# Gated linear attention and eight experts on one core: the second product of experts 3 to 7 by Strassen's seven products, in steps of 256 tokens

## The chip, the cores and the metric

The kernel runs on one NeuronCore of a Trainium2 chip. The metric is the time of one execution on the device, in microseconds (us); less is better. The kernel before took 1843.33 us, the median of three runs (1843.16 to 1844.97).

Engines are named as in the profile: PE does matrix products (PEld is its weight load), DVE and ACT do elementwise work, POOL does elementwise work on SBUF only, SP issues most DMAs. PE writes only to PSUM; DVE and ACT read and write PSUM and SBUF.

## The reference

Two parts. A recurrent attention over 4 batches, 8 heads, 768 tokens and head size 48 gives x, 3072 tokens by 384 columns. Then eight experts work on every token, and their results are mixed with weights P:

```python
def _attn_ref(q, k, v, alpha):
    ...
    for t in range(S):
        state = alpha[:, :, t, :, None] * state + np.einsum('bhd,bhe->bhde', k[:, :, t], v[:, :, t])
        y[:, :, t] = np.einsum('bhd,bhde->bhe', q[:, :, t], state)

def _moe_ref(x, w_gate, w1, w2):
    N, D = x.shape              # 3072, 384
    E = w_gate.shape[1]         # 8, and w1 is (8, 384, 1024), w2 is (8, 1024, 384)
    logits = x @ w_gate
    logits = logits - logits.max()
    P = np.exp(logits)
    for _ in range(8):
        P /= P.sum(1, keepdims=True) + 1e-09
        P /= P.sum(0, keepdims=True) + 1e-09
        P *= N / E
    out = np.zeros((N, D), dtype=np.float32)
    for e in range(E):
        h = np.maximum(x @ w1[e], 0.0)
        ye = h @ w2[e]
        out += P[:, e:e + 1] * ye
```

Every token goes through every expert, so nothing is gathered: each expert is two dense products, 3072 x 384 x 1024 (the first product) and 3072 x 1024 x 384 (the second).

## The kernel before

**Number format.** Each operand of the experts' products is held as two f16 tensors, a high part and a low part (index 0 and 1 of `h`, `w1`, `w2`, `xT`). A product of two such operands takes three passes (`PASSES`: high x high, high x low, low x high), all added in PSUM. `split` makes the two parts: ACT scales and rounds to the high part, DVE subtracts to get the low part.

**Early stage.** The attention is done in 24 chunks of 128 tokens, prepared by 12 blocks of 256 tokens. A block is a chain that goes back and forth between POOL (products `tmp`) and DVE (sums into `AB`), and ends with a round trip through DRAM. PE has little attention work, so the experts 0, 1 and 2 (`NA = 3`) are worked on meanwhile, as filler: `moe_tile` generators are pushed on the list `filler`, 256 tokens each, as soon as the tokens' x and the expert's weights are there, and `fill(us)` advances the first one by so many estimated microseconds of PE work. The order of everything up to the eighth chunk is written out by hand in the string `START`: `c0` advances chunk 0 by one step, `b2` block 2, `w1` the weights of expert 1, `d2` the decays of unit 2, `f` calls `fill(0.45)`; a capital letter puts some of that step's work on POOL instead of DVE. A loop with `FILL` orders the rest. In this stage `hold` pins all engines to the order in which the code is written. The unweighted results of experts 0 to 2 go to DRAM (`raw`), since P is known only at the end of the attention.

**Sinkhorn.** `sinkhorn` makes P: eight rounds, each a short chain of DVE operations, a product on PE, and DVE again. What is left of the filler runs beside it, and the weights of expert 3 are loaded and split.

**Late stage.** Experts 3 to 7, one after the other, in tiles of 512 tokens, also by `moe_tile`: for each of the 8 slices f of 128 hidden units, 9 matmuls 512 columns wide, ACT's relu into the high part of h, DVE's relu-and-subtract into the low part; then for each of the 4 token tiles of 128, 24 matmuls 384 columns wide into one PSUM tile, which `evac_add` multiplies by P and adds to `acc`. For expert 3 `evac_first` first reads the three `raw` results of that token tile back (`ri`) and adds them. While expert e runs, `load_expert(e + 1)` loads and splits the next weights, one step for each step of `moe_tile`. The products are pinned in their order by `mm`; DVE, ACT and SP are ordered by the framework's scheduler here. PSUM tiles: `psm` (4 banks), `psa` (2) and `psb` (2), all kept to the end.

The lines that matter: `PASSES` and `moe_tile`, `load_expert`, `fill` and `filler`, `sinkhorn`, and the last loop over `range(NA, E)`.

Of the kernel before, what the change touches and what calls it, by code (L numbers as in the profile page):

```python
# [8 lines left out]
F16 = mybir.dt.float16  # L9
# [14 lines left out]
def tile_gla_moe(ctx: ExitStack, tc: tile.TileContext, q, k, v, alpha, wg, w1, w2, out):  # L24
    nc = tc.nc
# [13 lines left out]
    START = 'c0 c1 f c0 f f f c1 W0 w0 f f c0 f c1 f f f f f w0 c0 f f W0 w0 f f f f f f c0 f f f c1 w0 f w0 c1 c0 f f f f w1 f w0 f f w0 f f w0 c1 w0 f w0 W1 f f c0 c2 f f f c2 f c1 f g c1 c0 c3 f f c1 f f W0 c0 f W0 f w0 f c2 c3 f f c1 f c1 f W0 c0 g c2 f w1 f f c0 W1 f f c3 w1 g f f c2 W1 f c3 c2 c1 f f f c3 w1 w0 f f f c2 f f f w1 c3 f f f c2 f f f f f f f w1 c3 f f W1 c3 f w1 f f f f f f f f f c3 w1 f c2 w1 b2 w1 w1 f f f W1 f c2 f f b2 f f f f f f c2 f f f f f f B2 f w1 f B2 f c2 c3 f f f b2 f f f f c3 c3 f f f f B2 f B2 b2 f f f f f f f f B2 f f f f f f f f f f f f f b2 f f b2 f f B2 B2 B2 f f f f b2 f f B2 f f f f f f f f f f f f f f f f c4 d2 f f f f f c4 f f f B3 b3 f f b3 c0 c4 f f f f f b3 b3 b3 b3 b3 f f f f f b3 w2 c5 f f f f f b3 f f f f f b3 w2 c4 f f f f f f b3 f f f f f b3 w2 c5 f f f f f b3 f f f f f b3 w2 c4 f f f f f f b3 f f f f f w2 c5 f f f f f f f f f f w2 d3 c6 f f f f f f f f f f f b4 w2 c5 f f f f f b4 f f f f f b4 w2 c6 f f f f f b4 f f f f f f b4 w2 c5 f f f f f b4 f f f f f b4 w2 c6 f f f f f b4 f f f f f b4 w2 c7 f f f f f f b4 f f f f f b4 w2 c6 f f f f f b4 f f f f f b4 w2 c7 f f f f f f b4 f f f f f b4 w2 c6 f f f f f b4 f f f f f w2 c7 f f f f f f f f f f f w2 d4 c8 f f f f f f f f f f b5 c7 f f f f f b5 f f f f f f b5 c8 f f f f f b5 f f f f f b5 c7 f f f f f b5 f f f f f b5'.split()  # L39
# [25 lines left out]
    def mm(out_, lhsT, rhs, start=True, stop=True):  # L65
        tc.keep_in_program_order(nc.tensor.matmul(out_, lhsT, rhs, start=start, stop=stop))  # L66
# [47 lines left out]
    def root_scale(sq, target, nm):  # L114
# [7 lines left out]
        VE.tensor_scalar_mul(p, p, 2.0 ** 64)  # L122
# [37 lines left out]
    def load_expert(e, pool, res):  # L160

        todo, pws = [], []
        for nm, w, target, C, W in (("w1", w1, W1T, KT_, FF), ("w2", w2, W2T, FT, DM)):
# [713 lines left out]
    while len(filler) > 3:  # L877
        fill(0.1)
# [65 lines left out]
```

## Time and profile before

| | |
|---|---|
| median of three runs | 1843.33 us |
| the profiled execution | 1843.05 us |
| its span, first to last instruction | 1841.3 us |
| mean granted clock of TensorE | 0.982 |
| PE busy | 1745.6 us, 14774 matmuls |
| DVE busy | 840.4 us |
| ACT busy | 541.9 us |

The profile comes from one execution. Its page gives the busy time of each engine over the whole span, and the span in 40 slices of 46 us. The views used below are: stretches (busy time of each engine in a window, with the number of instructions), groups (instructions of one shape: busy time, mean duration of one, idle time before them and what ended it), the timeline (instructions in order, equal ones merged, with idle time in square brackets), and the chain that ended last. A matmul's recorded duration includes the time to run out of the array, which the next one overlaps; its cost in a stream is the distance between the starts of groups.

### The profile page before, as it was taken

What the parts mean: (1) busy time and instruction counts of PE and PEld (TensorE: products, weight loads), DVE (VectorE), ACT (ScalarE), POOL (GpSimd) and SP (SyncE); (2) the same over time, 40 slices, a digit from 0 to 9 for tenths busy, and PEclk for the clock granted to TensorE, in tenths of its full rate; (3) what the DMA queues carried; (4) which work ended last, traced back from release to release, by engine and by line L of the source; (5) the groups of instructions that cost most, each with busy time, mean ns of one, the idle gap of its engine ahead of it and who ended that gap; (6) DMA issues with size and microseconds to landing.
All of it is one profiled execution on the core that took longest, in us unless ns stands there. A gap on an engine that the chain in (4) does not pass through costs nothing.

```text
span 1841.3 us, 34101 instructions
## 1 busy us (share of the span) xinstructions
PE 1745.6 (95%) x14774; PEld 1132.8 (62%) x14774; DVE 840.4 (46%) x1851; ACT 541.9 (29%) x1221; POOL 297.4 (16%) x270
## 2 busy tenths in 40 slices
PE   5899488999999999998999999999999999999999
PEld 5776466777777777776554555555555555555555
DVE  6465576666566556336465233222422242222222
ACT  5453243334333333325442123111411121111111
POOL 1124444445335424200000000000000000000000
PEclk9999598999999999999999999999999999999999
DMA  6114503431330432022362002000200000000000
GB/s 174 37 41 97 145 21 82 98 74 44 94 93 19 102 94 62 25 95 78 123 195 86 1 1 69 1 1 1 69 1 1 1 1 1 1 1 19 34 18 35
DMA packets 148198, 98.13 MB, mean 53 GB/s; under 512 B 107216, under 2 KB 138192, under 8 KB 148048
## 3 DMA queue, kind: packets, MB, share of 16 engines
q1 hardware_dynamic: 148048, 95.95, 18.8%
q8 instruction: 116, 1.90, 0.4%
q14 instruction: 34, 0.28, 0.1%
HBM read 67.63 MB, written 28.30 MB: 52 GB/s over the span
## 4 chain that ended last, share of the span: by engine, by line
PE 78%; DVE 10%; ACT 4%; DMA 4%; issue 2%; POOL 1%; SPq 0%; ACTq 0%; DVEq 0%; POOLq 0%
PE ps L66 70%; PE psy L66 3%; PE psl L66 2%; DMA ri<-raw 2%; DVE AB L57 2%; POOL tmp L57 1%; DVE tmp L57 1%; DVE deck L57 1%; DVE decq L57 1%; DVE h L57 1%; PE pss L66 1%; DVE w L57 1%; ACT junk L57 1%; ACT w L57 1%; ACT A L57 1%
## 5 line engine op out<-in xcount | busy, mean ns | idle before, releaser
L66 PE MATMUL ps<-xT,w 128*128 128x256 f16 (+2 forms) x4824 | 777.8, 320 | 16.8 <-DVE h L57 13.1
L66 PE MATMUL ps<-w,h 128*128 128x384 f16 x4608 | 774.1, 327 | 10.7 <-DVE h L57 9.8
L66 PEld LDWEIGHTS <-w 128*128 128x128 f16 x4824 | 467.7, 99 | 304.7 <-issue 20.1
L66 PEld LDWEIGHTS <-h 128*128 128x128 f16 x4608 | 450.0, 98 | 306.0 <-issue 9.7
L57 ACT ACTIVATE h<-ps 128x256 f16<-128x256 f32 (+2 forms) x536 | 251.6, 475 | 800.1 <-PE ps L66 799.6
L57 DVE SCALAR_TENSOR_TENSOR h<-ps,h 128x256 f16<-128x256 f32 (+2 forms) x536 | 280.9, 537 | 434.6 <-ACT h L57 434.2
L57 DVE SCALAR_TENSOR_TENSOR acc<-ps,pe,acc 128x384 f32<-128x384 f32 x120 | 74.1, 617 | 307.6 <-PE ps L66 307.6
L57 POOL TENSOR_TENSOR tmp<-qt,kt 128x768 f32<-128x768 f32 (+2 forms) x81 | 141.5, 1752 | 153.1 <-DVE AB L57 66.0
L57 DVE TENSOR_REDUCE AB<-tmp 128x16 f32<-128x768 f32 (+2 forms) x90 | 81.1, 902 | 42.0 <-POOL tmp L57 41.8
L57 ACT COPY r<-ps 128x384 f32<-128x384 f32 x72 | 34.4, 477 | 149.4 <-PE ps L66 139.7
L57 ACT COPY A<-psl 16x128 f32<-16x128 f32 (+4 forms) x164 | 52.5, 327 | 53.4 <-PE psl L66 51.9
L66 PE MATMUL psy<-vn,A 128*128 128x48 f32 x384 | 58.2, 283 | 1.7 <-issue 1.7
L66 PE MATMUL psl<-Tq,Tk 48*32 48x16 f32 (+3 forms) x2752 | 46.1, 191 | 13.9 <-DVE A L57 6.0
L66 PEld LDWEIGHTS psy<-vn,A 128*128 128x128 f32 x384 | 54.9, 209 | 2.1 <-issue 2.0
L66 PEld LDWEIGHTS psl<-Tq,Tk 48*32 48x32 f32 (+2 forms) x2752 | 40.7, 114 | 23.9 <-issue 8.7
L57 ACT ACTIVATE ys<-psy,s_t 128x384 f32<-128x384 f32 x24 | 14.0, 581 | 104.0 <-DVE s_t L57 79.4
L57 POOL TENSOR_TENSOR kt<-kt,al 128x384 f32<-128x384 f32 x40 | 41.1, 1028 | 2.6
L57 POOL TENSOR_TENSOR A<-an,mask 128x1024 f32<-128x1024 f32 x20 | 40.0, 2000 | 0.0
L57 DVE TENSOR_TENSOR qt<-qt,al 128x384 f32<-128x384 f32 (+1 forms) x50 | 39.6, 792 | 0.0
L57 DVE SCALAR_TENSOR_TENSOR acc<-ri,pe,acc 128x384 f32<-128x384 f32 x48 | 29.5, 616 | 21.4 <-DMA ri<-raw 18.3
L57 DVE TENSOR_REDUCE mx<-psy 128x1 f32<-128x384 f32 x24 | 13.3, 555 | 56.7 <-PE psy L66 56.7
L66 PE MATMUL psy<-ST,Tq 128*128 128x96 f32 x160 | 35.6, 306 | 2.9 <-DVE lg L57 1.8
(160 smaller groups left out, 965.0 us busy)
## 6 DMA issues: line engine op xcount, KB each, us to landing
raw<-r SPq DMA_DIRECT2D x72, 192.0 KB, 1.9
ri<-raw SPq DMA_DIRECT2D x72, 192.0 KB, 2.4
w1f<-in_moe_w_dram SPq DMA_DIRECT2D x5, 1536.0 KB, 6.4
w2f<-in_moe_w_dram SPq DMA_DIRECT2D x5, 1536.0 KB, 7.3
vn<-in_v_dram SPq DMA_DIRECT2D x24, 192.0 KB, 3.6
xT<-in_moe_w_dram SPq DMA_DIRECT2D x6, 768.0 KB, 6.7
out_dram<-acc SPq DMA_DIRECT2D x24, 192.0 KB, 1.9
qt<-in_q_dram SPq DMA_DIRECT2D x10, 384.0 KB, 5.4
```

What stands on the lines that cost most here:

```text
L57: r = f(*a, **k_)
L66: tc.keep_in_program_order(nc.tensor.matmul(out_, lhsT, rhs, start=start, stop=stop))
```

## The change

Three things change.

**1. The second product of experts 3 to 7.** A step is 256 tokens, that is two token tiles of 128. The second product is seen as a 2 x 2 block product: two token tiles, two halves of the hidden units (4 slices of 128 each), two halves of the output columns (192 each). Strassen's method (in Winograd's form) needs seven block products in place of eight, each 4 slices x 3 passes = 12 matmuls 192 columns wide. It needs sums of blocks: of h (four DVE operations for each of the 4 slices pairs, `hf` 4 to 7, before the split into two f16 parts, which now makes 7 x 128 = 896 columns in place of 512), and of w2 (four subtractions, once an expert, in `load_late`). Sums of the products are made in PSUM: ACT copies product X into Y, and DVE writes X + v into Z, and later products are added on top of what was written there. `acc` now takes five additions of 192 columns a step.

**2. The order of the late stage.** The seven products of a step stand between the four pieces of the next step's first product (`F` is 18 matmuls 256 columns wide). The `raw` results are read back one expert at a time: expert 0's beside expert 3, 1's beside 4, 2's beside 5. `load_late` takes the place of `load_expert`: one staging buffer in place of two (first w1, then w2), and more empty steps between its parts.

**3. The order of the early stage.** `START` is a new string: 640 entries in place of 571, 459 `f` in place of 390, `B3`, `B4` and `B5` in place of some `b3`, `b4` and `b5`. Filler left at the start of `sinkhorn` is sorted by expert, and the loading of expert 3 begins inside that part. The three PSUM pools are closed before the late stage, and two new ones opened (`psm2`, 3 banks; `psv`).

Scales of the sums of squares change by powers of two, with no new instruction.

```diff
-    START = 'c0 c1 f c0 f f f c1 W0 w0 f f c0 f c1 f f f f f w0 c0 f f W0 w0 ...'.split()
+    START = 'c0 c0 f f c1 c0 f c1 f f f f f f c1 f f W0 f f f f c0 f f f W0 W0 ...'.split()
...
+    filler[1:] = sorted(filler[1:], key=lambda x: x[0])
+    w3_ = load_late(NA)
+    advance(w3_, 1)
     for n, _ in enumerate(sinkhorn()):
         fill(2.8 if n else 4.0)
-    while len(filler) > 3:
-        fill(0.1)
+        if n > 1:
+            advance(w3_, 1)
     while filler:
-        advance(w3_, 1)
-        fill(1.0)
+        if all(e for e, _ in filler):
+            advance(w3_, 1)
+        fill(2.0)
...
+    def load_late(e):
...
+        def staged(nm, w, target):
+            t = wst.tile([P, KT_ * FF], F32, tag="wst", name=f"{nm}f_{e}")
...
+            SP.dma_start(t.rearrange("p (c f) -> p c f", f=src.shape[2]), src)
+            yield from [None] * 3
...
+                SE.activation(junk, t[:, i * n:(i + 1) * n], AF.Square, scale=2.0 ** 16, accum_out=ss[:, i:i + 1])
...
+            yield from [None] * 2
...
+        for c in range(KT_):
+            split(t[:, c * FF:(c + 1) * FF], sc, *(x[:, c] for x in w1h))
+            yield
+        t, pw2, sc = yield from staged("w2", w2, W2T)
...
+        def put(n, src):
+            split(src, sc, *(x[n // 4][:, n % 4] for x in q))
+
+        put(0, b11)
+        yield
+        VE.tensor_sub(b11, b12, b11)
+        put(3, b11)
+        yield
...
+    T = 2 * P
...
+    def first(e, t0):
...
+        for j in range(HF):
+            ps = psm.tile([P, 2, T], F32, tag="psm", name=f"ps1_{e}_{t0}_{j}")
+            for z in range(2):
+                f = j + z * HF
...
+                        mm(ps[:, z], w1h[i][:, c, f * P:(f + 1) * P], xs(k_, c, t0, T),
+                           start=(n == 0), stop=(n == 3 * KT_ - 1))
...
+            SE.activation(a[:, :4].rearrange("p (z r) t -> p z (r t)", z=2), ps, AF.Relu)
+            VE.tensor_add(a[:, 4], a[:, 0], a[:, 2])
+            VE.tensor_sub(a[:, 5], a[:, 4], a[:, 1])
+            VE.tensor_sub(a[:, 6], a[:, 1], a[:, 0])
+            VE.tensor_sub(a[:, 7], a[:, 3], a[:, 5])
+            hi, lo, src = (x.rearrange("p n t -> p (n t)") for x in (h[0][:, j], h[1][:, j], a[:, 1:]))
+            SE.copy(hi, src)
+            VE.tensor_sub(lo, src, hi)
+            yield
+
+    def second(e, t0):
...
+        def prod(o, a, b, start=False):
+            n = 0
+            for f in range(HF):
+                wf = w(b, f)
+                for (i, k_) in PASSES:
+                    mm(o, h[i][:, f, a], wf[k_], start=start and n == 0, stop=n == 3 * HF - 1, skip_group_check=True)
+                    n += 1
...
+        prod(V, 3, 3, True)
+        v = hp2.tile([P, HD], F32, tag="v", name=f"v_{nm}")
+        SE.copy(v, V)
+        yield
+        prod(X, 0, 0, True)
+        SE.copy(Y, X)
+        yield
+        prod(X, 4, 4)
+        VE.tensor_add(Z, X, v)
+        add(t2, hi_, v)
+        yield
+        prod(Y, 2, 1)
+        yield
+        prod(X, 5, 5)
+        add(t2, hi_, X)
+        yield
+        prod(Z, 6, 2)
+        add(t1, lo_, Y)
+        add(t1, hi_, Z)
+        yield
+        prod(X, 1, 6)
+        add(t2, lo_, X)
...
+        F = first(*todo[n + 1]) if n + 1 < len(todo) else iter(())
+        new = second(e, t0)
+        for i, a in enumerate((F, F, old, new, new, F, new, F, new, new, new)):
+            next(a, None)
+            if i % 3 == 1:
                 next(more, None)
-        ws = wn
+        old = new
+    advance(old, 99)
```

How the instructions stand on the engines follows, at three places.

DVE in the late stage, expert 5, before: the end of the tile of tokens 1024 to 1535. `h1` is the low part of h, `pe` the weight P of a token tile, `acc` the result.

```order
L57 SCALAR_TENSOR_TENSOR h1_5_1024_14976<-ps1_5_1024_6_15049,h0_5_1024_14975 128x512
L57 SCALAR_TENSOR_TENSOR h1_5_1024_14976<-ps1_5_1024_7_15061,h0_5_1024_14975 128x512
L57 SCALAR_TENSOR_TENSOR acc_10652<-ps2_5_1024_0_15073,pe_5_8_15098,acc_10652 128x384
L57 TENSOR_TENSOR pe_5_12_15308<-PR_10653,wsc_85 128x1
L57 SCALAR_TENSOR_TENSOR acc_10652<-ps2_5_1024_1_15101,pe_5_9_15126,acc_10652 128x384
```

The same engine and tokens in the changed kernel: about half of one step, from the first piece of tokens 1024 to 1279 on; the second product there is that of tokens 768 to 1023.

```order
L57 TENSOR_TENSOR hf_5_1024_0_17780<-hf_5_1024_0_17780 128x128 x4
L57 SCALAR_TENSOR_TENSOR acc_10664<-ps2x_5_512_17616,pe_5_4_17608,acc_10664 128x192
L57 TENSOR_TENSOR hf_5_1024_1_17807<-hf_5_1024_1_17807 128x128 x3
L57 TENSOR_TENSOR pe_5_8_18061<-PR_10665,wsc_85 128x1
L57 TENSOR_TENSOR hf_5_1024_1_17807<-hf_5_1024_1_17807 128x128
L57 TENSOR_TENSOR h1_5_1024_17760<-hf_5_1024_0_17780,h0_5_1024_17759 128x896
L57 SCALAR_TENSOR_TENSOR acc_10664<-v_5_768_17858,pe_5_6_17835,acc_10664 128x192
L57 TENSOR_TENSOR h1_5_1024_17760<-hf_5_1024_1_17807,h0_5_1024_17759 128x896
L57 TENSOR_TENSOR hf_5_1024_2_17892<-hf_5_1024_2_17892 128x128 x3
L57 TENSOR_TENSOR ps2z_5_768_17845<-ps2x_5_768_17843,v_5_768_17858 128x192
```

Where one DVE operation of 512 columns followed each slice of the first product, there are now four of 128 and one of 896 for each pair of slices, and the writes to `acc` and to the PSUM tile Z stand between them.

ACT in the late stage of the changed kernel, one step of expert 5 (before, ACT had one relu of 512 columns for each slice, and nothing that PE's second product waited for in PSUM):

```order
L57 ACTIVATE hf_5_2304_0_18921<-ps1_5_2304_0_18902 128x512
L57 ACTIVATE hf_5_2304_1_18948<-ps1_5_2304_1_18929 128x512
L57 CAST h0_5_2304_18900<-hf_5_2304_0_18921 128x896
L57 CAST h0_5_2304_18900<-hf_5_2304_1_18948 128x896
L57 COPY v_5_2048_18999<-ps2v_5_2048_18983 128x192
L57 COPY ps2y_5_2048_18985<-ps2x_5_2048_18984 128x192
L57 ACTIVATE hf_5_2304_2_19033<-ps1_5_2304_2_19014 128x512
L57 CAST h0_5_2304_18900<-hf_5_2304_2_19033 128x896
```

The copy of X into Y stands behind two casts, which stand behind DVE's sums for the same pieces.

DVE in the early stage, before, where chunk 5 (`0_5`) has its decays: `AB1` and `tmp` belong to the block of batch 1, and `deck32` is what PE's `psl` of chunk 5 needs.

```order
L57 TENSOR_REDUCE AB1_121<-tmp4_1_0_14_2712 128x4x4
L57 TENSOR_TENSOR qt_1_0_2608<-qt_1_0_2608,al_1_0_2610 128x2x192
L57 TENSOR_TENSOR al_1_0_2610<-al_1_0_2610 128x2x48
L57 TENSOR_TENSOR tmp8_1_0_15_2731<-qt_1_0_2608,kt_1_0_2609 128x1536
L57 TENSOR_TENSOR decq32_0_5_2753<-Tq_0_5_2751,q32_0_128 128x256
L57 TENSOR_TENSOR deck32_0_5_2755<-Tk_0_5_2744,k32_0_130 128x256
```

The same place in the changed kernel:

```order
L57 TENSOR_REDUCE AB1_121<-tmp4_1_0_14_2684 128x4x4
L57 TENSOR_TENSOR qt_1_0_2431<-qt_1_0_2431,al_1_0_2433 128x2x192
L57 TENSOR_TENSOR al_1_0_2433<-al_1_0_2433 128x2x48
L57 TENSOR_REDUCE AB1_121<-tmp8_1_0_15_2703 128x4x8
L57 TENSOR_TENSOR decq32_0_5_2760<-Tq_0_5_2758,q32_0_128 128x256
L57 TENSOR_TENSOR deck32_0_5_2762<-Tk_0_5_2751,k32_0_130 128x256
```

The product `tmp8` has gone to POOL, and its sum on DVE now stands ahead of chunk 5's decays instead of behind them.

More of the change, by code (lines that the diff above doesn't have):

```diff
@@ L63, in tile_gla_moe, with mm @@
     VE, SE, GE, SP = (Held(x) for x in (nc.vector, nc.scalar, nc.gpsimd, nc.sync))
-    def mm(out_, lhsT, rhs, start=True, stop=True):
-        tc.keep_in_program_order(nc.tensor.matmul(out_, lhsT, rhs, start=start, stop=stop))
+    def mm(out_, lhsT, rhs, start=True, stop=True, **k_):
+        tc.keep_in_program_order(nc.tensor.matmul(out_, lhsT, rhs, start=start, stop=stop, **k_))
     def tr(out_, in_, idn):
@@ L710, in fill @@
             try:
-                owed[0] -= next(filler[0])
+                owed[0] -= next(filler[0][1])
             except StopIteration:
@@ L729, in tile_gla_moe @@
     wAB = [[] for _ in range(NA)]
-    w0, w1_, w2_ = (load_expert(e, None, wAB[e]) for e in range(NA))
+    w0, w1_, w2_ = (load_expert(e, wAB[e]) for e in range(NA))
     wgf = cp.tile([P, KT_, E], F32, name="wgf")
@@ L744, in push @@
     def push(*tiles):
-        filler.extend(moe_tile(e, wAB[e], t0, T, hp1, evac_raw) for e, t0, T in tiles)
+        filler.extend((e, moe_tile(e, wAB[e], t0, T, hp1, evac_raw)) for e, t0, T in tiles)
     steps = [0] * len(chunks)
@@ L884, in tile_gla_moe @@
     early.close()
+    attn_ps.close()
     hp2 = ctx.enter_context(tc.tile_pool(name="hp2", bufs=2, side="right"))
-    T = 512
-    def evac_first(e, tt, ps):
-        for i in range(NA):
-            r = rp.tile([P, DM], F32, tag="raw", name=f"ri{i}_{tt}")
-            SP.dma_start(r, raw[i][tt * P:(tt + 1) * P])
-            pt = sm.tile([P, 1], F32, tag="pe0", name=f"pe{i}_{tt}")
-            VE.tensor_mul(pt, PR[:, tt, i:i + 1], wsc[:, i:i + 1])
-            if i == 0:
-                SE.activation(acc[:, tt], r, AF.Copy, scale=pt)
-            else:
-                VE.scalar_tensor_tensor(acc[:, tt], r, pt, acc[:, tt], op0=ALU.mult, op1=ALU.add)
-        evac_add(e, tt, ps)
@@ L902, in evac_add @@
-    def evac_add(e, tt, ps):
-        pt = sm.tile([P, 1], F32, tag="pe", name=f"pe_{e}_{tt}")
-        VE.tensor_mul(pt, PR[:, tt, e:e + 1], wsc[:, e:e + 1])
-        VE.scalar_tensor_tensor(acc[:, tt], ps, pt, acc[:, tt], op0=ALU.mult, op1=ALU.add)
-        if e == E - 1:
-            SP.dma_start(out[tt * P:(tt + 1) * P], acc[:, tt])
-    for e in range(NA, E):
-        wn = []
-        more = load_expert(e + 1, wst, wn) if e + 1 < E else iter(())
-        for t0 in range(0, NT, T):
-            for _ in moe_tile(e, ws, t0, T, hp2, evac_first if e == NA else evac_add):
+    psm = ctx.enter_context(tc.tile_pool(name="psm2", bufs=3, space=PSUM))
@@ new lines, in tile_gla_moe @@
+    for x in "yz":
+        mm(psv.tile([P, 256], F32, tag=x, name=f"bits{x}")[:, :HD], ident.bitcast(F16)[:, :P],
+               xT[0][0][:, 0, :HD])
+    todo = [(e, t0) for e in range(NA, E) for t0 in range(0, NT, T)]
+    advance(first(*todo[0]), 99)
+    old = iter(())
+    for n, (e, t0) in enumerate(todo):
+        if t0 == 0:
+            more = load_late(e + 1) if e + 1 < E else iter(())
+        F = first(*todo[n + 1]) if n + 1 < len(todo) else iter(())
[3 more added lines that the diff above has]
+            if i % 3 == 1:
```

140 lines of the change are left out of this document (104 added, 36 removed).

## The prediction

> **What bounds the kernel now.** I read the page first, then a table of stretches, then the timeline where a price is needed. In the page, the 40 slices:
>
> ```profile
> PE   5899488999999999998999999999999999999999
> DVE  6465576666566556336465233222422242222222
> ACT  5453243334333333325442123111411121111111
> PEclk9999598999999999999999999999999999999999
> ```
>
> PE is full from slice 7 on; DVE and ACT are at a quarter in the last half. Two stretches of the late stage and three of the early one (columns: PE, PEld, DVE, ACT, POOL busy, then the granted clock):
>
> ```profile
> 150.00:200.00 50.00, 34.26 (x437) 25.97 (x436) 28.92 (x49) 13.44 (x38) 26.53 (x21) 0.86 0.54 149
> 200.00:250.00 50.00, 37.81 (x372) 30.53 (x373) 29.64 (x65) 20.92 (x55) 18.01 (x15) 0.73 0.34 79
> 250.00:300.00 50.00, 39.22 (x470) 30.76 (x468) 32.74 (x61) 18.24 (x48) 19.00 (x15) 0.83 0.33 78
> 962.00:993.00 31.00, 27.76 (x146) 13.89 (x145) 21.09 (x59) 8.80 (x16) 0.00 (x0) 1.00 0.51 153
> 1334.00:1365.00 31.00, 31.00 (x169) 16.37 (x168) 8.65 (x16) 4.78 (x8) 0.00 (x0) 1.00 0.00 1
> ```
>
> In the late stage PE never rests and the clock is whole: only fewer PE columns, or a new wait, can change its length. Expert 3 alone loses a little (962 to 993), to the reading back of `ri`. How long the late stage is, from the timeline's first 512-wide group and the chain's last pieces:
>
> ```profile
> 895.62 4.70 PE L66 MATMUL ps<-xT,w 128*128 128x512 f16 x21
> 1109.21 177.13 PE ps L66 x957
> 1296.32 177.13 PE ps L66 x957
> 1483.43 354.27 PE ps L66 x1920
> ```
>
> It runs from 895.62 to 1483.43 + 354.27 = 1837.70: 942.1 us. One expert takes 1296.32 - 1109.21 = 187.11.
>
> **The price of a matmul.** Distances between the starts of groups:
>
> ```profile
> 872.15 7.96 PE L66 MATMUL ps<-w,h 128*128 128x384 f16 x48
> 879.96 8.02 PE L66 MATMUL ps<-xT,w 128*128 128x256 f16 x72
> 887.82 7.96 PE L66 MATMUL ps<-w,h 128*128 128x384 f16 x48
> 103.23 1.17 PE L66 MATMUL ps<-xT,w 128*128 128x128 f16 x18 [0.19 <-DVE h L57]
> 690.20 0.37 PE L66 MATMUL psg<-wg,xT 128*128 128x8 f16 x9
> 690.42 3.11 PE L66 MATMUL ps<-xT,w 128*128 128x256 f16 x27
> ```
>
> 384 columns: 7.81 / 48 = 162.7 ns. 256 columns: 7.86 / 72 = 109.2 ns. 128 more columns cost 53.5 ns, so 192 should cost 109.2 - 26.8 = **82.4 ns**, a form that this trace does not have. Its bounds: 128 columns took at most 1.17 / 18 = 65 ns, 256 took 109. The weight load is not what limits it: `psg` loads nine full 128 x 128 weights for 8 columns each and takes 0.22 us, 24 ns a pair.
>
> **The late stage, PE alone.** A step of 256 tokens has 4 x 18 = 72 matmuls of 256 columns, 7.86 us, and 7 x 12 = 84 of 192, 6.92 us: 14.78 us. 60 steps (5 experts of 12): 887 us. Against 942.1 that is **-55**, of which 6.5 is expert 3's loss (942.1 - 5 x 187.11), which I take as gone: each expert reads 24 `ri` tiles now and not 72, and DVE has them asked for a step ahead.
>
> **What DVE and ACT add, and whether it hides.** The rows:
>
> ```profile
> L57 DVE TENSOR_TENSOR PR<-PR,ri 128x192 f32<-128x192 f32 x8 | 2.9, 358 | 0.3
> 178.59 0.96 DVE L57 TENSOR_TENSOR qt<-qt,al 128x768 f32<-128x768 f32 x1
> 832.44 1.08 DVE L57 SCALAR_TENSOR_TENSOR h<-ps,h 128x256 f16<-128x256 f32 x3
> L57 DVE SCALAR_TENSOR_TENSOR h<-ps,h 128x256 f16<-128x256 f32 x35 | 14.0, 421 | 17.5 <-ACT h L57 17.5
> L57 DVE SCALAR_TENSOR_TENSOR acc<-ps,pe,acc 128x384 f32<-128x384 f32 x120 | 74.1, 617 | 307.6 <-PE ps L66 307.6
> L57 DVE TENSOR_TENSOR pe<-PR,wsc 128x1 f32<-128x1 f32 x183 | 27.5, 158 | 5.2 <-ACT acc L57 1.3
> L57 DVE SCALAR_TENSOR_TENSOR w<-w1f,s_w,w 128x768 f16<-128x768 f32 x16 | 15.8, 1013 | 3.0 <-ACT w L57 3.0
> L57 ACT ACTIVATE h<-ps 128x512 f16<-128x512 f32 x239 | 141.8, 595 | 646.5 <-PE ps L66 646.4
> L57 ACT COPY r<-ps 128x384 f32<-128x384 f32 x72 | 34.4, 477 | 149.4 <-PE ps L66 139.7
> L57 ACT CAST w<-xT 128x768 f16<-128x768 f32 x5 | 4.2, 832 | 0.2
> L57 ACT ACTIVATE PR<-lm 128x192 f32<-128x192 f32 x1 | 0.4, 362 | 4.2 <-DVE lm L57 4.2
> ```
>
> DVE, two-tensor operations: 358 ns at 192 columns, 960 at 768, so 1.045 ns a column; 128 columns 0.29 us, 896 columns 1.09. Per step: 16 sums of 128 (4.6), 4 low parts of 896 (4.4), 5 `acc` of 192 (617 - 200 = 0.42 each, 2.1), Z (0.36), two `pe` (0.3): **11.8 us** if nothing overlaps. Operations that don't wait for each other overlap: three `h` of 0.421 took 1.08, 0.09 less for each after the first; with 28 operations the sum could come down to 9.3. ACT: 4 relus (2.4), 4 casts of 896 (0.832 + 128 x 0.92 ns = 0.95, 3.8; 0.92 is (595 - 477) / 128), v and Y (0.7): 6.9. Both fit in 14.78, so on average all of it hides beside PE.
>
> Does it hide in order? One step by hand, us from its first matmul. PE: two pieces of the next first product to 3.9, the last product of the step before to 4.9, V to 5.9, X to 6.9, third piece to 8.9, X again to 9.8, fourth piece to 11.8, Y 12.8, X 13.8, Z 14.8. ACT casts pieces 0 and 1 once the last old product has released h (5.1), with v between: 5.1 to 7.4; then copies X to Y, 7.4 to 7.8. PE wants Y's copy done at 8.9: **1.1 us to spare**, the least in the step. DVE writes Z by 10.9, and PE adds to it from 13.8: 2.9 to spare. The low part of piece 3 ends at 16.7, and the next V needs it at 14.8 + 4.9 = 19.7: 3.0 to spare. So a plain step should run without a wait.
>
> **The steps that also load weights.** Per expert DVE splits 3 x 1024 columns of w1 (1.013 + 0.27 = 1.28 each), 7 blocks of 768 (1.013) and subtracts 4 of 768 (0.96). The last two, 10.9 us, come in seven consecutive advances, four a step: 6.2 us a step for 1.75 steps. 11.8 + 6.2 = 18.0 is 3.2 over PE's step; with the overlap (0.09 off each of the eleven) 9.3 + 5.7 = 15.0, barely over it. Experts 4 and 5 add two `ri` a step (2 x 0.617 and two `pe`, 1.55). And ACT's sums of squares may wait for the DMA with relus and the copy of Y behind them; in the trace such a wait was:
>
> ```profile
> 1310.28 0.84 ACT L57 ACTIVATE junk<-w2f 128x768 f16<-128x768 f32 x1 [5.23 <-DMA w2f<-in_moe_w_dram]
> ```
>
> Per load, bounds: nothing if the spare 1 to 3 us take it all up; 3.2 x 1.75 + 5.2 = 10.8 if none of it hides. I take 4, nearer to the low end since three pieces of first product stand in PSUM's three buffers ahead of any wait. Four loads: **+16** (0 to +43).
>
> **Ends of the stage.** The first step's first product has no partner; V waits for piece 3: relu 0.6, sums 1.0, cast 0.95, low part 1.1 and queues, about 4.6 against the 3.9 of two pieces; and the closing of the PSUM pools makes the first piece wait for the last `r` copy, 0.5. With the wait for weights still queued on DVE I take **+2** (0.5 to 4). The last step has no first product between its products: X into Y (0.6) and piece 3 (0.7) show: **+1**.
>
> **Sinkhorn.** PE waits there for the squares of expert 3's weights:
>
> ```profile
> 850.47 0.39 PE L66 MATMUL pst_w<-w1m,ones 128*128 128x4 f32 x2 [1.63 <-ACT junk L57]
> 860.46 0.39 PE L66 MATMUL pst_w<-w2m,ones 128*128 128x4 f32 x2 [2.75 <-ACT junk L57]
> ```
>
> 4.4 us. The empty steps ahead of that matmul, and squares begun earlier, should remove most: **-3.5** (-4.4 to 0; the rest of the chain is the same DVE work between the same filler).
>
> **The new START.** The same work on PE, in another order. In both orders the filler ahead of chunk 5's x is tokens 0 to 511 for experts 0 and 1 and no more: supply, not the string, sets the dry place at 187 to 260. What can move are waits like these:
>
> ```profile
> 199.03 1.93 PE L66 MATMUL psl<-decq,deck 48*32 48x32 f32 x48 [11.22 <-DVE deck L57]
> 259.15 2.08 PE L66 MATMUL ps<-w,h 128*128 128x384 f16 x6 [5.09 <-DVE h L57]
> ```
>
> The first ends when DVE, in its fixed order, gets past `tmp8` and its neighbours to `deck`. In the new order `tmp8` is on POOL, but its sum stands ahead of `deck`, so the same chain is waited for. Both gone is -16, the same again lost is +16; with the new order neither freed nor blocked in the rows, I take **-3**, near zero.
>
> **The sum.** 1843.05 (the profiled execution; span 1841.3 and 1.75 around it; the median is 0.3 above) - 55 + 16 + 2 + 1 - 3.5 - 3 = 1800.5: **1801 us**.
>
> **Rivals.**
> - *Everything hides.* The loads cost nothing: 1801 - 16 = **1785**, and down to 1772 with a START that gains. For it: the spare times above and DVE's overlap. Chance 0.18.
> - *DVE is the bound while weights load.* 10.8 a load: 1801 + 43 - 16 = **1828**. For it: 18.0 against 14.78. Against: those steps are 7 of 60. Chance 0.17.
> - *START loses.* The early waits double: 1801 + 19 = **1820**. Chance 0.02.
> - *Slower: the copy of Y is late in every step.* Place: ACT's copy of X into Y, behind two casts, which wait for DVE's sums. If that queue is later by 1.1 + d than my table, PE's second X product waits d, 60 times. From d = (1846.7 - 1801) / 60 = 0.76 it is slower than before; d = 1 gives **1861**. For it: 28 DVE operations in fixed order. Against: 80% of a step at most, and ACT at 47%. Chance 0.03.
> - *Slower: the weight load does not hide behind 192 columns.* The load's row says 98 ns:
>
> ```profile
> L66 PEld LDWEIGHTS <-h 128*128 128x128 f16 x2880 | 281.4, 98 | 194.7 <-DVE h L57 5.0 <-ACT h L57 1.5
> ```
>
>   Then a matmul is 98 - 82.4 = 15.6 ns dearer, 84 x 60 x 15.6 ns = 79: **1880**. Against: `psg` at 24 ns a pair and 128 columns at 65. Chance 0.02. The Trainium skill, in "TensorE: Matmul & The Clock Gate", section "Back-to-back issue gap", gives for a stream of loads and matmuls about 81 ns at 128 columns and 131 at 512; a straight line between them is an estimate of 89 ns at 192 by that page, with which the sum would be 1835. The trace disagrees with it at both ends: at most 65 ns at 128 and, from 1307.88 to 1323.41 for 72, 216 ns at 512:
>
> ```profile
> 1307.88 15.70 PE L66 MATMUL ps<-xT,w 128*128 128x512 f16 x72
> ...
> 1323.41 10.89 PE L66 MATMUL ps<-w,h 128*128 128x384 f16 x66
> ```
>
> **How the numbers follow.** My forecast, 1792 to 1813, has 0.58; the others as said. Range **1780 to 1825**: it takes in most of "everything hides" and about half of "DVE is the bound"; some 0.16 stays outside. Against a bound of 0.2% (3.7 us, about what a measurement of this kernel can tell from no change): faster 0.94, same 0.02, slower 0.04.
>
> **What would show it.** Late stage: the start-to-start of 84 matmuls of 192 columns (6.9 us); a plain step of 14.8 us; windows with weights 15 to 18 us a step, PE's wait there ended by ACT's Y or DVE's `ps2z` or h. Sinkhorn: no wait for `junk`. Early: first late matmul at about 889, 6.5 before 895.62. Wrong if a step without loading is longer than 15.2 us, or if the late stage starts more than 15 us off.

## The result, and the profile after

| | before | after |
|---|---|---|
| median | 1844.15 us (1843.16 to 1846.79, 4 runs) | 1776.10 us (1775.79 to 1777.48, 4 runs) |
| ratio, 95% interval | 1 | 0.963 [0.9614, 0.9647] |
| the profiled execution | 1843.05 us | 1775.87 us |
| its span | 1841.3 us | 1774.1 us |

The change gains 68 us. The forecast was 42, and the time lies 4 us below the range's lower end. The 40 slices of the page after the change (44 us each, busy tenths):

```profile
PE   6898899999999999999999999999999999999999
DVE  6475576556646746336679777987687677766666
ACT  5452543333333333324665545554455445444443
PEclk6698799999999999999999999999999999999999
```

DVE has gone from a quarter to between six and nine tenths in the late stage, and PE still looks full there. The 66 against 99 at the start of PEclk is no loss: the clock of the kernel before is on record only from 77 us on, and groups of the same shape last as long there (128 matmuls of `psl`, 16 columns wide, 2.34 us at 26.69 before and at 22.07 after). The digits hide the waits, since 9 begins at 90%, so marks in the timeline tell more. In the timeline, `gm` is the first operation of the Sinkhorn part; before:

```profile
814.76 0.34 DVE L57 TENSOR_REDUCE gm<-lg 128x1 f32<-128x192 f32 x1
```

After, in the same view, with the first matmul of the late stage and the last one of the kernel:

```profile
782.98 0.34 DVE L57 TENSOR_REDUCE gm<-lg 128x1 f32<-128x192 f32 x1
...
859.88 0.24 PE L66 MATMUL bitsy<-xT,ident 128*128 128x192 f16 x1 [0.61 <-ACT r L57]
...
1769.63 1.15 PE L66 MATMUL ps2x<-w,h 128*128 128x192 f16 x12
```

| part | before | after | measured | forecast |
|---|---|---|---|---|
| early stage, to `gm` | 814.76 | 782.98 | -31.8 | -3 |
| Sinkhorn, `gm` to the late stage | 80.9 | 76.9 | -4.0 | -3.5 |
| late stage, to PE's last end | 942.1 | 910.9 | -31.2 | -36 |
| from there to the span's end | 3.6 | 3.3 | -0.3 | 0 |

The first row is off by 29 us, the third by 5. The stretches of the early stage after the change (PE, PEld, DVE, ACT, POOL busy, granted clock, DMA share, GB/s), to be laid beside the three that the prediction shows:

```profile
150.00:200.00 50.00, 37.98 (x434) 30.63 (x431) 28.84 (x63) 16.27 (x46) 28.16 (x22) 0.76 0.53 148
200.00:250.00 50.00, 46.60 (x551) 36.20 (x552) 36.44 (x72) 27.47 (x69) 26.46 (x19) 0.90 0.30 67
250.00:300.00 50.00, 48.69 (x596) 39.76 (x595) 35.45 (x68) 18.37 (x51) 24.05 (x21) 1.00 0.37 90
```

Between 150 and 300 us PE was idle for 38.7 us before and is for 16.7 now, and the mean clock there rises from 0.81 to 0.89. In the second and the third stretch the clock rises as the rests shrink. In the first it falls from 0.86 to 0.76 though PE rests 3.7 us less, so the idle time of a stretch alone doesn't give its clock; the last section comes back to that.

In the late stage, the chain of work that ended last shows the plain step as the distance between equal pieces (start, duration):

```profile
1540.46 3.93 PE ps L66 x36
1555.26 3.93 PE ps L66 x36
1570.05 3.93 PE ps L66 x36
1584.84 3.93 PE ps L66 x36
```

14.79 us, as forecast from the columns. The groups (busy us, mean ns of one, idle before, who ended it) give the durations that the trace of before did not have, and the wait that is left:

```profile
L57 DVE TENSOR_TENSOR h<-hf,h 128x896 f16<-128x896 f32 x240 | 258.0, 1089 | 99.2 <-ACT h L57 98.6
L57 ACT CAST h<-hf 128x896 f16<-128x896 f32 x240 | 224.9, 937 | 210.5 <-DVE hf L57 173.2
L57 DVE TENSOR_TENSOR hf<-hf 128x128 f32<-128x128 f32 x960 | 234.0, 286 | 114.7 <-ACT hf L57 112.4
L66 PE MATMUL ps2x<-w,h 128*128 128x192 f16 x2880 | 276.8, 246 | 14.3 <-ACT ps2y L57 14.0
```

PE waits 14.0 us for ACT's copy of X into Y. The distances between the starts of V in successive steps tell what the loading steps cost in all: from 871.83 to 1763.14 there are 59 of them, 37 of 14.79 us, the last of 10.86 (the step that has no first product beside it); the first 58 sum to 880.45, which is 22.6 over 58 x 14.79. How one such place looks, first on ACT (timeline; the last bracket is idle time and what ended it):

```profile
1283.62 0.84 ACT L57 ACTIVATE junk<-w2f 128x768 f16<-128x768 f32 x1 [2.83 <-DMA w2f<-in_moe_w_dram]
...
1289.42 0.94 ACT L57 CAST h<-hf 128x896 f16<-128x896 f32 x1
1290.26 0.31 ACT L57 COPY ps2y<-ps2x 128x192 f32<-128x192 f32 x1
```

and on PE:

```profile
1285.95 2.13 PE L66 MATMUL ps<-xT,w 128*128 128x256 f16 x18
1290.63 1.15 PE L66 MATMUL ps2x<-w,h 128*128 128x192 f16 x12 [2.55 <-ACT ps2y L57]
1291.62 3.79 PE L66 MATMUL ps<-xT,w 128*128 128x256 f16 x18
1295.25 1.15 PE L66 MATMUL ps2y<-w,h 128*128 128x192 f16 x12
```

A square of the next weights waits 2.83 us for its DMA. Behind it in ACT's order stand three more squares, two relus, two casts, the copy of V and the copy of Y; PE waits 2.55, and then 18 matmuls that otherwise show 2.13 us show 3.79. Another place has no square near it. There a split of the next w2 waits on ACT for DVE's subtraction, and the copy of Y stands behind it:

```profile
1149.16 0.94 ACT L57 ACTIVATE w<-w2f,s_w 128x768 f16<-128x768 f32 x1 [2.10 <-DVE w2f L57]
...
1153.53 0.31 ACT L57 COPY ps2y<-ps2x 128x192 f32<-128x192 f32 x1
```

```profile
1153.89 1.15 PE L66 MATMUL ps2x<-w,h 128*128 128x192 f16 x12 [1.20 <-ACT ps2y L57]
```

### The profile page after: what moved, and what is told of

Its sections match the earlier page's. It is cut to its first block, busy times and chain, and to the rows that moved or that the text cites. A ratio compares the mean times of both kernels' runs of the same rounds, so it can differ in the third digit from the quotient of the medians.

```text
span 1774.1 us, 44644 instructions
## 1 busy us (share of the span) xinstructions
PE 1698.3 (96%) x19096; PEld 1477.6 (83%) x19096; DVE 1192.2 (67%) x3080; ACT 798.0 (45%) x1591; POOL 298.6 (17%) x271
## 4 chain that ended last, share of the span: by engine, by line
PE 64%; DVE 19%; ACT 6%; DMA 4%; issue 3%; POOL 3%; SPq 1%; ACTq 0%; POOLq 0%; DVEq 0%
PE ps L66 40%; PE ps2x L66 9%; DVE h L57 3%; PE psy L66 3%; DVE hf L57 3%; PE psl L66 2%; DVE w L57 2%; PE ps2y L66 2%; PE ps2z L66 2%; POOL tmp L57 2%; PE ps2v L66 2%; ACT h L57 2%; DVE AB L57 2%; DVE acc L57 1%; DMA w2f<-in_moe_w_dram 1%
## 5 line engine op out<-in xcount | busy, mean ns | idle before, releaser
L66 PE MATMUL ps<-xT,w 128*128 128x256 f16 (+1 forms) x6984 | 809.5, 273 | 11.7 <-DVE h L57 9.3
L66 PEld LDWEIGHTS <-w 128*128 128x128 f16 x6984 | 677.4, 99 | 94.4 <-issue 15.0
L66 PEld LDWEIGHTS <-h 128*128 128x128 f16 x6768 | 588.9, 98 | 130.3 <-issue 21.9
L57 DVE TENSOR_TENSOR h<-hf,h 128x896 f16<-128x896 f32 x240 | 258.0, 1089 | 99.2 <-ACT h L57 98.6
L57 ACT CAST h<-hf 128x896 f16<-128x896 f32 x240 | 224.9, 937 | 210.5 <-DVE hf L57 173.2
L57 DVE TENSOR_TENSOR hf<-hf 128x128 f32<-128x128 f32 x960 | 234.0, 286 | 114.7 <-ACT hf L57 112.4
L66 PE MATMUL ps<-w,h 128*128 128x384 f16 x1728 | 296.6, 327 | 2.9 <-DVE h L57 2.9
L66 PE MATMUL ps2x<-w,h 128*128 128x192 f16 x2880 | 276.8, 246 | 14.3 <-ACT ps2y L57 14.0
L57 ACT ACTIVATE hf<-ps 128x512 f32<-128x512 f32 x240 | 142.2, 593 | 194.4 <-PE ps L66 187.0
L57 DVE SCALAR_TENSOR_TENSOR h<-ps,h 128x256 f16<-128x256 f32 (+1 forms) x296 | 114.0, 411 | 133.9 <-ACT h L57 133.1
```

The lines of the kernel that those rows point to most:

```text
L57: r = f(*a, **k_)
```

## The experiments

In all of them "changed kernel" is the kernel after the change; each was measured beside the kernel before on the same chip. The chips differ a little (the kernel before took 1842.4 to 1844.7 us on them), so between two runs of different chips a few microseconds are not read as a difference; the ratios are safer.

**1. Is START worth 31 us? From both sides.** First the changed kernel with the old string:

```diff
-    START = 'c0 c0 f f c1 c0 f c1 f f f f f f c1 f f W0 ...'.split()
+    START = 'c0 c1 f c0 f f f c1 W0 w0 f f c0 f c1 f f f ...'.split()
```

> The changed kernel with the string START of before; all else as changed. Theory A (my forecast was short because of START): START is worth about 32 us, since gm comes at 782.98 us after the change and at 814.76 before it; this run should give 1776 + 32 = 1808 us, with gm near 815 us. Rival B (START is worth the 3 us of my forecast, and the lead at gm came of other edits, such as the squares with a scale or the filler list): 1779 us.

Measured: 1807.34 us (1807.06 to 1809.28), ratio to before 0.9806 [0.9788, 0.9824]; `gm` at 816.20. Theory A. The mirror is the kernel before with the new string:

> The kernel before with the new string START; the last stage as before. Theory A: 1844 - 32 = 1812 us, the mirror of the run before. Rival B: 1841 us. Rival C (the lead needs the new late stage to be kept, for example since the old one waits for weights at its start): a lead at gm of about 30 us of which much less is left at the end.

Measured: 1812.71 us (1811.24 to 1815.36), ratio 0.9838 [0.9815, 0.986]; `gm` at 783.03. Theory A again: the string alone is worth 31 us beside the new late stage and 30 beside the old one (1842.44, the median of before on that chip, to 1812.71), so next to nothing of the lead is lost later.

**2. Which part of START?** The old string up to the last step of chunk 3 (its first 209 entries), then three steps of block 2 that the new string has earlier, and behind them the new one's entries from its 263rd on:

> The changed kernel, START with the order of before up to the last step of chunk 3 (209 entries) and from there on the new order. Marks of after against before: 8 us ahead at the decays of unit 2 (154.38 against 162.78), 18 at chunk 5's x (200.7 against 218.8), 31 at the decays of unit 4. Theory A (two sources: the head gives 8, the new order of the dry place 24): 1776 + 8 = 1784 us. Rival B (the head's lead is what grows, since a dry place comes to lie otherwise): 1800 to 1808 us. Rival C (the rest alone makes it): 1776 us.

Measured: 1784.45 us (1782.95 to 1787.38). Theory A. The next cut is at the decays of unit 3 (`d3`):

> The changed kernel, START in the order of before up to the decays of unit 3 (d3, its entry 377) and from there on the new order, with the four entries that the new order has ahead of d3 (a step each of chunks 5 and 6, unit 4 and expert 2) directly behind it. The run with the old order and the one with the old order only up to chunk 3 reach these decays at the same time (217.63 and 216.91) and the next ones 66.4 and 51.6 us later: their 23 us arise behind d3. Theory A (it is what the entries behind d3 do: the next decays' steps then reach VectorE with filler between): 1783 to 1790 us. Rival B (what stands ahead of d3 decides: chunk 5's x, 4 us ahead of d3 rather than 4 us behind it, gives 768 columns of filler that everything behind lives on): 1800 to 1807 us.

Measured: 1791.88 us (1788.00 to 1795.44). That is 2 us above theory A's range and 8 below the rival's: half of the gain arises behind `d3`. Then the two complements:

> The changed kernel, START in the new order up to the decays of unit 3 and in the order of before behind them: the complement of the run with the old order up to there (1791.88 us). Theory A (the parts of START add: 8.4 us up to chunk 3, 7.4 to the decays of unit 3, 15.5 behind them): 1776.1 + 15.5 = 1792 us, within 3. Rival B (a lead ahead of unit 3 is what the rows behind live on, so the complement keeps more or less than its part): 1785 or less, or 1800 or more.

Measured: 1791.49 us (1789.18 to 1795.53).

> The changed kernel, START in the new order up to chunk 3's last step and in the order of before from there on: the complement of the run with the old order up to chunk 3 (1784.45 us). Theory A (the parts add): 1807.3 - 8.4 = 1799 us, within 3. Rival B (they do not): 1776 to 1792 us, or 1804 and more.

Measured: 1801.35 us (1800.15 to 1803.45). All six together:

| up to chunk 3 | to `d3` | behind `d3` | median us | ratio to before, 95% interval |
|---|---|---|---|---|
| new | new | new | 1776.10 | 0.963 [0.9614, 0.9647] |
| old | new | new | 1784.45 | 0.9682 [0.9662, 0.9701] |
| new | new | old | 1791.49 | 0.9719 [0.9695, 0.9744] |
| old | old | new | 1791.88 | 0.972 [0.9696, 0.9745] |
| new | old | old | 1801.35 | 0.9772 [0.9755, 0.979] |
| old | old | old | 1807.34 | 0.9806 [0.9788, 0.9824] |

The steps from one row to the next, 8.35, 7.43 and 15.46, make up the 31.24 by construction; the test is the two complements, which come within 0.1 and 2.4 us of the sums of these parts. So the parts add, within some 2 us: it is not one lead that grows. For the part behind `d3`, the stretch 220 to 290 us (PE busy, granted clock, DMA share, GB/s), in the run with the old string:

```profile
220.00:290.00 70.00, 55.49 (x588) 0.82 0.29 67
```

and in the run with the old string up to `d3` and the new one behind:

```profile
220.00:290.00 70.00, 67.08 (x839) 0.96 0.31 77
```

PE rests 14.5 us in the first and 2.9 in the second, and the clock goes from 0.82 to 0.96: 11.6 of the 15.5 us are idle time; the rest fits matmuls at a lowered clock, which was not tested by itself. In the run with the old string, the timeline of PE names the waits:

```profile
201.49 1.93 PE L66 MATMUL psl<-decq,deck 48*32 48x32 f32 x48 [9.56 <-DVE deck L57]
...
225.98 6.35 PE L66 MATMUL ps<-xT,w 128*128 128x256 f16 x44 [2.69 <-DVE xT L57]
261.11 2.08 PE L66 MATMUL ps<-w,h 128*128 128x384 f16 x6 [5.09 <-DVE h L57]
284.07 0.58 PE L69 MATMUL psd<-ident,DN 16*128 16x16 f32 x4 [5.40 <-DMA DN<-ds]
```

(`DN` is what comes back from DRAM at the end of a block.) The last two are the waits of 5.09 and 5.61 us at 259.15 and 282.60 of the kernel before. With the new order behind `d3` neither of them is there. But the part is not the price of these two waits: in the complement, the new order up to `d3` and the old one behind it, h is waited for less than 1 us and DN for 2.24, another wait has come in their place, and the loss against the changed kernel is the same 15 us:

```profile
252.05 2.02 PE L66 MATMUL pss<-vn,kb 128*128 128x96 f32 x8 [4.92 <-DVE g_w L57]
```

Which single entry of the string removes which wait was not tried.

**3. Or is it GpSimd's share?** The order rows ahead of the prediction show `tmp8` moved from DVE to POOL. The new order with the old choice between the two engines, for example behind the decays of unit 2:

```diff
-    d2 b3 b3 B3 b3 c4 b3 B3 f f c0
+    d2 b3 b3 b3 b3 c4 b3 b3 f f c0
```

> The changed kernel, START in its new order, but the choice between VectorE and GpSimd (upper case) of each block and weight step as the same step has it in the START of before: of the units' products B3 1 instead of 9, B4 0 instead of 6, B5 0 instead of 4, B2 9 instead of 8. Theory A (the order makes the lead): within 4 us of 1776. Rival B (the share that GpSimd takes of the decays' tables makes it, since VectorE sets the pace from 150 to 300 us): 1790 to 1808 us.

Measured: 1777.24 us (1776.71 to 1778.28), ratio 0.9641 [0.9624, 0.9658]. Theory A: in the new order the choice is worth about 1 us. And the old order with the new choice:

> The changed kernel, START in the order of before, but with the new order's choice between VectorE and GpSimd for each block and weight step (B3 9 instead of 1, B4 6 and B5 4 instead of 0). With the old order the two longest waits there, 9.56 us for deck at 201.49 and 5.09 us for h at 261.11, each stand behind a product tmp of 3.45 us on VectorE. Theory A (that product on VectorE, in the old order, is what those waits are made of, though in the new order it hardly matters): about 10 us less than 1807, 1795 to 1800 us. Rival B (the tables' chain is waited for all the same, on GpSimd): 1804 to 1810 us.

Measured: 1802.72 us (1802.43 to 1807.66), ratio 0.9786 [0.9766, 0.9806], between the two theories: 4.6 us less than with the old choice, on another chip, where the two intervals still overlap. The wait for deck falls from 9.56 to 6.33, the wait for h stays at 5.08. So the order made nearly all of the gain, and the engine at most some 5 us of it, in the old order alone.

**4. What do the waits for Y stand behind?** Six empty steps instead of three between a tensor's DMA and its squares; advances three times a step instead of four; both:

```diff
-            yield from [None] * 3
+            yield from [None] * 6
             ss = sm.tile([P, 4], F32, tag="wm", name=f"{nm}m_{e}")
...
-            if i % 3 == 1:
+            if i in (1, 5, 9):
                 next(more, None)
```

> The changed kernel, late stage: six empty steps instead of three between a weight tensor's DMA and its squares. Theory A (the squares' wait for the DMA, 11.7 us on ScalarE in five waits, holds up the copy of Y, and with it TensorE: 14.0 us of waits in 13 places and about 7 us at a lowered clock after the two longest): TensorE's waits for Y fall below 5 us and the time to 1760 to 1766 us. Rival B (VectorE's splits and subtractions are what delays the casts ahead of Y's copy): the waits stay at 11 to 16 us and the time within 3 us of 1776.

> The changed kernel, late stage: the next expert's weights advanced three times a step instead of four, in the 2nd, 6th and 10th of its eleven places. That lengthens the time between DMA and squares from 11.1 to 14.8 us and spreads the splits over four steps a tensor in place of three. Theory A (the squares' wait for the DMA is the cause): about half to all of the 14 us of waits go, 1762 to 1770 us. Rival B (VectorE's load in the steps with splits): the same or more, 1758 to 1766 us, and more than in the run with six empty steps. Theory C (neither): 1776 us.

> The changed kernel, late stage with both: six empty steps and three advances a step. If the two causes add (A and B each hold in part): the least of the three runs, about 1756 us (1776 less 14 us of waits and 7 us of lowered clock is 1755). If one cause carries all: the same as the better of the two other runs, within 2 us.

Then two kinds of instructions pinned among themselves, with three and with six empty steps:

```diff
-                SE.activation(junk, t[:, i * n:(i + 1) * n], AF.Square, scale=2.0 ** 16, accum_out=ss[:, i:i + 1])
+                pin(nc.scalar.activation(junk, t[:, i * n:(i + 1) * n], AF.Square, scale=2.0 ** 16, accum_out=ss[:, i:i + 1]))
...
-        SE.copy(Y, X)
+        pin(nc.scalar.copy(Y, X))
```

> The changed kernel with only two kinds of ScalarE's instructions of the late stage pinned to the order of the code among themselves: the squares of the weights and the copy of Y, so that no square is put ahead of a copy of Y that stands before it in the code; three empty steps. Theory A (a square that waits for its DMA ahead of the copy of Y is the cause of TensorE's waits): they fall from 14.0 us to 4 or less, and the time to 1757 to 1764 us, below the 1766.8 of six empty steps alone. Rival B (VectorE's splits, subtractions and ri sums delay the casts ahead of the copy): waits of 8 us or more stay in the steps with splits, 1766 to 1772 us.

> As the run before, with six empty steps as well. Theory A: within 3 us of the run before, and the least of all runs if the w2 squares still wait for their DMA there (2.8 us each with three empty steps). Rival B: the same as six empty steps alone, 1764 to 1770 us.

And six empty steps with the copy on the other engine:

```diff
-        SE.copy(Y, X)
+        VE.tensor_copy(Y, X)
```

> Six empty steps, nothing pinned, and the copy of X into Y on VectorE instead of ScalarE (60 copies of about 0.36 us more there, 10 to 11.2 of 14.79 us busy before). Theory A (ScalarE's queue is what makes Y late): the waits for Y go to 3 us or less, 1755 to 1762 us. Rival B (VectorE's queue is as late, with splits ahead of the copy): the waits become waits for VectorE's Y of 8 us or more, 1764 to 1780 us.

| run | median us (lowest to highest) | ratio to before, 95% interval | PE's waits for Y, us | 58 steps over 14.79, us |
|---|---|---|---|---|
| changed kernel | 1776.10 (1775.79 to 1777.48) | 0.963 [0.9614, 0.9647] | 14.0 | 22.6 |
| six empty steps | 1766.77 (1764.96 to 1769.82) | 0.9583 [0.9566, 0.96] | 7.5 | 12.9 |
| three advances | 1769.65 (1765.53 to 1770.71) | 0.9593 [0.9575, 0.961] | 9.1 | 16.3 |
| both | 1768.26 (1766.27 to 1769.41) | 0.9587 [0.9569, 0.9605] | 7.0 | 15.5 |
| pinned, three empty | 1768.16 (1766.24 to 1771.94) | 0.9589 [0.9574, 0.9604] | 8.6 | 14.8 |
| pinned, six empty | 1766.81 (1764.97 to 1769.49) | 0.958 [0.9566, 0.9594] | 4.4 | 12.2 |
| six empty, Y on DVE | 1778.31 (1775.94 to 1782.96) | 0.9643 [0.9623, 0.9664] | 14.1 | 25.1 |

Both causes hold, and the splits weigh more than the squares. In the changed kernel's trace, two of the 13 waits, 4.0 of the 14.0 us (2.55 at 1290.63 and 1.40 at 1473.93), have squares ahead of the copy that waited for their DMA. In eight, 7.9 us, a split of the next weights stands there that waited on ACT for DVE, for the scale of w1 or for a subtraction in w2. The rest is the reading back of `raw` (1.62 at 894.24) and two short ones.

The runs agree with that. With pinned squares and copies no square waits for its DMA any more, and 8.6 us of waits stay: rival B of that run. Four of its eight waits, of about 1 us each, stand behind a subtraction, and the longest, 3.32 us, behind squares that did not wait. With six empty steps the squares wait about as long as before (11.4 us in place of 11.7 on ACT): the scheduler still puts the squares of the next w1 right behind the DMA,

```profile
996.75 0.84 ACT L57 ACTIVATE junk<-w1f 128x768 f16<-128x768 f32 x1 [3.65 <-DMA w1f<-in_moe_w_dram]
```

and three such places make 6.2 of the 7.5 us that are left. What has gone there is nearly every wait behind a split, since the splits have moved to other places of the steps. With both, pinned and six empty steps, 4.4 us stay, none over 1.5. Each of these five runs brings 6 to 9 us, and they can't be told from one another by their times. Theory A's numbers mostly failed: six empty steps came out 1 us above its range, the pinned run 4 us, and six empty steps with three advances 12 us above the sum that was made for them, which counted 7 us of lowered clock where it is 3.3. DVE is no better place for the copy: there the waits are 14.1 us again (rival B). Six empty steps, in one changed line, beat both kernels: the interval of that run lies wholly below the changed kernel's.

**5. What does the copy of Y cost when it is late in every step?** The prediction had that as a rival. Pinning everything in the late stage to the order of the code brought it about, though not it alone:

```diff
     advance(w3_, 99)
-    hold[0] = False
     early.close()
```

> The changed kernel with its late stage's instructions on ScalarE, VectorE and SyncE also pinned to the order of the code, as in the early stage (three empty steps, four advances). In the run with six empty steps a weight's squares still came right behind its DMA (waits of 3.65 and 2.54 us for w1f), since the scheduler puts them ahead of where the code has them. Theory A (that is where the rest of the waits comes from): no wait of a square for a DMA over 0.5 us, TensorE's waits for Y 3 us or less, 1757 to 1763 us. Rival B (pinned order costs as much elsewhere, as VectorE's and ScalarE's queues then have no overlap made by the scheduler): 1770 to 1785 us.

Measured: 1979.00 us (1977.27 to 1982.00), ratio 1.0733 [1.0712, 1.0754]. Both theories' numbers were far off. PE's waits in the late stage of that run (total, times, longest):

```profile
PE ps2x L66 <- ACT ps2y L57: 101.1, 60, 6.2
PE ps2x L66 <- DVE ps2z L57: 64.2, 45, 5.0
```

60 waits for 60 steps, 1.7 us each, and the writing of Z behind them; no step is shorter than 16.07 us but the last. With six empty steps as well:

> The changed kernel with both: late stage pinned to the order of the code, and six empty steps. Theory A: the same as with the pinned order alone within 2 us, if no square waits for its DMA there; 3 us or more below it if the DMA, issued behind VectorE's last split, still lands later than 11 us after its place in the code. Rival B: as in the run before, 1770 to 1785 us.

Measured: 1988.48 us (1987.30 to 1989.96), ratio 1.0788 [1.077, 1.0806]; 9 us worse, where pinned squares and copies alone were not. The order that the scheduler gives to ACT, DVE and SP, not the code's, is what hides Strassen's sums. Since all three engines were pinned, 1979 us is not the price of a late Y by itself.

## Why the prediction was wrong, point by point

- **PE's price: right.** 192 columns were forecast at 82.4 ns from the distance between 128, 256 and 384; the step of 14.79 us gives (14.79 - 7.86) / 84 = 82.5. The rival in which the weight load shows falls with it. The Trainium skill's 81 and 131 ns in "TensorE: Matmul & The Clock Gate", section "Back-to-back issue gap", from which the prediction made an estimate of 89, don't hold for this stream.
- **DVE's and ACT's durations: right.** 1089, 937 and 286 ns against 1.09, 0.95 and 0.29 us forecast. Plain steps ran without a wait.
- **Loads, +16: right in place, a little short in size.** The waits are at the copy of Y, as the prediction's step by hand had it (the least to spare). It named both causes: DVE's load in the steps with splits, which is behind 7.9 of the 14.0 us, and the square that waits for its DMA (its row of 5.23 us), behind 4.0. The 58 steps ran 22.6 us over, of which 13.7 are waits for Y, 3.3 the lowered clock behind the two longest of them, and 1.4 the waits for V of the first step; the rest is in pieces of 0.3 us or less. The prediction priced waits only, not the clock after them. The late stage as a whole came out 4.8 us above its terms.
- **Head +2, tail +1, Sinkhorn -3.5: right** (waits for V of 0.40, 0.18 and 0.79 and one of 0.61 for the last `r` copy; 0.39 for the last Y; -4.0).
- **START, -3 (-16 to +16): wrong, and it made the prediction wrong.** It measured -31.8, and the late stage started 29 us ahead of its mark of 889, which the prediction itself named as a sign of being wrong. Two statements failed. "Supply, not the string, sets the dry place at 187 to 260": the string also sets when the supply comes (the first `psx` of chunk 5's x is at 200.73 after and at 218.76 before), and with a supply as late as before (217.54, the run with the old string up to `d3`) the entries behind `d3` alone still brought 15.5 us. And the bound was drawn from the two longest waits, 11.22 + 5.09, though the stretches quoted at the top of the prediction showed 38.7 us of idle PE at a mean clock of 0.81 between 150 and 300: a gain of all of it was open, with some of the clock's loss beside it. Up to `gm`, PE's idle time fell from 80.4 to 53.9 us, which is 26.5 of the 31.8, 22.0 of them between 150 and 300. The claim that the chain to `deck` is waited for all the same held in the old order (9.56, with POOL's share 6.33), not in the new one, where that wait is 1.37.
- **The rivals.** "Everything hides" named 1772 with a START that gains, and the time is near it, but its mechanism isn't what happened: the loads did not hide. "The copy of Y is late in every step" is a true mechanism that this kernel escapes by its scheduler; forced, with the whole order, it costs 1.7 us a step for Y and 1.1 for Z in waits alone, more than the 1 us a step at which it was priced.

The sum again, with what was measured in the place of the terms: 1800.5 - 28.8 (START) - 0.5 (Sinkhorn) + 4.8 (late stage) - 0.3 (end) = 1775.7; the profiled execution took 1775.87.

## What to carry to other kernels

When a change gives a stage a new hand-written order, bound its gain by all the idle time of the bottleneck engine in that stage, and by the work that runs at a lowered clock there, not by the waits that one can name. Where one engine's in-order queue holds both a short operation that the bottleneck waits for and an operation that waits for a DMA, keep the second far behind its transfer, and look in the trace whether the scheduler has left it there. And a price from the differences between widths in the same trace is worth more than a general one.

## What the runs showed of the hardware

**The clock follows windows of 3.41 us: a rest of 2 us within one costs half the speed of the next.** Fourteen of the profiles share this late stage, up to the order of some instructions (the changed kernel, the seven other runs with the new late stage of the first three experiments, and the six of the fourth). In them PE waited 88 times for 0.9 us or more, from the second step on. None of the 61 waits under 2 us was followed by slower matmuls. Of the 27 from 2.01 to 3.32 us, 16 were and 11 were not, so the length of a wait does not decide it. With six empty steps a wait of 2.81 us cost only itself:

```profile
1002.12 1.15 PE L66 MATMUL ps2x<-w,h 128*128 128x192 f16 x12 [2.81 <-ACT ps2y L57]
1003.11 2.13 PE L66 MATMUL ps<-xT,w 128*128 128x256 f16 x18
```

and in the run with pinned squares and three empty steps one of 3.32 us slowed what followed:

```profile
894.87 1.52 PE L66 MATMUL ps2x<-w,h 128*128 128x192 f16 x12 [3.32 <-ACT ps2y L1024]
896.19 3.46 PE L66 MATMUL ps<-xT,w 128*128 128x256 f16 x18
```

In each of these traces the granted clock changes only at whole multiples of 3.41 us from its other changes, and each of the 16 falls is one such window at 0.50. Laid on these windows, the wait of 2.55 us at 1290.63 of the changed kernel and the one of 2.81 with six empty steps look so (window, PE busy, granted clock, DMA share, GB/s):

```profile
1288.24:1291.66 3.42, 1.03 (x13) 1.00 0.00 0
1291.66:1295.07 3.41, 3.41 (x19) 0.50 0.02 5
```

```profile
997.84:1001.26 3.42, 1.47 (x14) 1.00 0.23 58
1001.26:1004.67 3.41, 2.55 (x27) 1.00 0.22 58
```

In the first, 2.38 us of the wait lie in one window, and the next is at half clock. In the second the wait is split, 1.95 and 0.86, and the clock stays. Of the 27 waits, the 15 with more than 2.00 us within one window all had a fall; of the 12 others one did, with 1.99. How little a window may hold when the matmuls are small was not worked out. A fall costs about 1.7 us: at 1290.63 of the changed kernel the next 30 matmuls take 4.62 us from start to start, where a plain step has 2.96. The Trainium skill, in "TensorE: Matmul & The Clock Gate", section "What's actually happening", says that the clock is lowered after an idle window of about 3.4 us. By that rule all of these waits would be free. The runs disagree: all 16 waits with a fall were shorter than that, 14 of them 2.71 us or less.

**DVE and POOL hold each other up.** In the run with the old string, DVE's product ahead of the late h, and what follows it:

```profile
254.66 3.45 DVE L57 TENSOR_TENSOR tmp<-qt,kt 128x1536 f32<-128x1536 f32 x1
258.03 2.02 DVE L57 TENSOR_TENSOR decq<-Tq,q 128x256 f32<-128x256 f32 x1
```

while POOL had

```profile
254.59 1.91 POOL L57 TENSOR_TENSOR A<-an,mask 128x1024 f32<-128x1024 f32 x1
256.46 3.31 POOL L57 TENSOR_TENSOR tmp<-qt,kt 128x768 f32<-128x768 f32 x1
```

In the run with the old string up to chunk 3, POOL rested beside the same DVE product until its last 0.1 us:

```profile
242.83 1.75 DVE L57 TENSOR_TENSOR tmp<-qt,kt 128x1536 f32<-128x1536 f32 x1
```

1.75 us alone and 3.45 beside POOL's 1.91: the one runs after the other. The Trainium skill says so in "SBUF — State Buffer", section "SBUF: two separate sides": the two engines share a pair of ports that one of them holds for a whole instruction. These rows agree. The two operations ahead of the late h are 1.70 and 1.61 us longer than alone (1.75, and 0.41 for a product of the same shape, `decq` at 260.31); how much of PE's 5.09 us would go without it was not tried.
